# Loads in runs of one token, a chunk's state one step later, and half of the second group's first layer by twenty products, in a gated-recurrence and SiLU-MLP kernel on Trainium2

## The chip, the cores and the metric

The kernel runs on one core of one Trainium2 chip. The metric is the time of one execution in device microseconds: before the change 556.75 us, the median of three runs (555.87 to 556.92). All of the profile is of one further execution, which took 557.26 us; the span from its first to its last instruction is 555.5 us, with TensorE's granted clock at 0.999.

## The reference

A gated linear recurrence over 4 batches, 8 heads, 768 tokens and 48 dimensions a head, and then a two-layer block with SiLU on the 3072 rows of 384 that it gives. All is float32.

```python
for t in range(S):                                   # B, H, S, D = 4, 8, 768, 48
    state = alpha[:, :, t, :, None] * state + einsum('bhd,bhe->bhde', k[:, :, t], v[:, :, t])
    y[:, :, t] = einsum('bhd,bhde->bhe', q[:, :, t], state)
x = y.transpose(0, 2, 1, 3).reshape(B * S, H * D)    # 3072 x 384
h = x @ w_in                                         # 384 x 2048
out = (h * (1.0 / (1.0 + exp(-h)))) @ w_out          # 2048 x 384
```

## The kernel before

**Chunks and steps.** The recurrence is cut into 24 chunks of 128 tokens: chunk n is piece n // 4 of batch n % 4. For a chunk the kernel needs, per head, running products of alpha along the tokens (two scans on VectorE, L734 for u and L764 for p), `kp = k * u` (L749, L751) and `qp = q * p` (L770, written over p), a 128 x 128 matrix of scores `kp^T qp` on TensorE (L388, ps_a<-p,kp), which ScalarE copies out (L818, L821) and GpSimd masks to its causal half (L825), values from scores and v and from the carried state (ps_a<-g,vn and ps_a<-p,st), and the new state from kn and v (ps_a<-vn,kn), added on VectorE (L880). kn is kp turned: tokens on the partitions.

The loop at the end of `quotients` runs over steps. A step has four slots; the table `stages` says which parts of which chunk stand in a slot: in the later half (from step NA = 8) scores of chunk n-1 in slot 0, products of chunk n in slot 1 (alpha's turn, u, k's turn, kp), quotient in slot 2 (p, q's turn, qp), values and states of chunk n-1 and the flip of chunk n in slot 3. After each slot `fill` adds work of the two-layer block. TensorE's order is that of the program; the order on the other engines is settled by the scheduler that builds the kernel, save where `keep_in_program_order` is called.

**How a chunk gets in.** In the first eight steps a, k and q are loaded with tokens on the partitions and turned by TensorE. From chunk 8 on they are loaded into three tiles at, kt and qt (one each) in a form in which VectorE can turn them in blocks of 32 x 32: partition b of a block of 32 holds, for each head, four tokens in a row, 4b to 4b + 3, in one run of 768 bytes; a second load of the same data stands 32 floats further left on the next 32 partitions, so that dimensions 32 to 47 come to lie where the turn of the second half finds them. `turned` (L708) reads 32 floats for each token and writes every fourth float of its target, because of the token order. Each of the three loads is 4 DMAs on SP's queue (L486), issued when the turn of the chunk before has freed the tile.

**kn.** `flip` turns kp on VectorE (L780) into a tile `turn`, which also holds k's and q's turned forms, and stores it to DRAM (L782); `land` loads it back as kn, by 4 DMAs on SP's queue (L790), at the start of the next step.

**The two-layer block.** 3072 rows are six groups of 512; a group has two halves h of 256 rows (two chunks each). xt holds a half's rows turned. The first layer makes 16 blocks of 128 columns, in two pairs of 8 blocks: `pair` 0 and 1. Groups 0 and 1 take it plainly (`enter_plain`): for 2 blocks at a time 6 matmuls of 256 columns into a PSUM bank, and a SiLU by ScalarE (L923). Groups 2 to 5 take it by `enter`: 20 products of combined blocks for both halves together in place of 24, two matmuls each, in seven pieces; ScalarE copies PSUM banks out (L950), VectorE combines them (L958 and L587), ScalarE takes SiLUs of pairs of blocks (L955). Such products need 11 sums of token blocks (`sums_x`, tile xc) for each group, and 23 sums of w_in's blocks (`sums_w`, in w_in and a tile wx) for each pair, once. The second layer (`leave`) makes each half's output by 7 products, each 8 matmuls of 192 columns into ps_o, after a side-by-side sum of SiLU blocks (`side_by_side`, L1033) and differences (L1047); GpSimd's queue stores the result (L1059).

**Pieces.** `pieces` lists all pieces with a weight (12) and the chunk up to which values must be there; `fill` takes as many as are due by a schedule of marks. For group 1, pair 1 there are eight plain pieces, interleaved with the seven of `leave(0, 1)`. `done` inside `leave` also calls `sums_w`: pair 0 in `leave(0, 1)`, pair 1 in `leave(1, 0)`, four sums a piece.

PSUM: three banks for the first layer (ps_m), two for the second (ps_o), three for the recurrence (ps_a).

Of the kernel before, what the change touches and what calls it, by code (L numbers as in the profile page):

```python
# [9 lines left out]
I32 = mybir.dt.int32  # L10
# [345 lines left out]
def quotients(  # L356
# [109 lines left out]
    def load(n, names="akq"):  # L466
        if n == NT:
            return
        c = ctxs.setdefault(n, dict(zip(("ci", "b"), divmod(n, B))))
        b, rows = c["b"], slice(c["ci"] * C, c["ci"] * C + C)  # L470
        for name, src in (("a", alpha), ("k", k), ("q", q)):
            if name not in names:
                continue
            x = src[b, :, rows, :]
            if n < NA:
                c[name] = nat[name][n % NIN]
                nc.sync.dma_start(c[name][:, :, 0:D], x.transpose([1, 0, 2]))
                continue

            c[name] = late["quads"][name]
            for u in range(2):
                for i in range(2):
                    r = 64 * u + 32 * i
                    nc.sync.dma_start(  # L486
                        c[name][r : r + 32, 32 * (1 - i) :][:, 0 : 4 * NP * D].rearrange(
                            "p (g c) -> p g c", g=NP),
                        x[u::2].rearrange("h (b j) d -> b h (j d)", j=4))

    NV = 2
    vns = [fix.tile([128, H, 64], F32, name=f"vn{i}") for i in range(NV)]
# [164 lines left out]
    def audit():  # L657


        flat = alpha.rearrange("b h s d -> (b h s d)").rearrange("(p c) -> p c", p=128)  # L660
        assert 2 * HD <= 32 + 4 * NP * D
        todo = [(flat[:, c : c + AW], AW, 0) for c in range(0, flat.shape[1], AW)]
        if wide:
            todo += [(moe_w_in[t * 128 : t * 128 + 128, c : c + 512], 512, 1)
                     for c in range(0, DF, 512) for t in range(NKT)]
            todo += [(moe_w_out[f * 128 : f * 128 + 128, :], HD, 1) for f in range(NFT)]
        alone = sum(2 * x[1] > 32 + 4 * NP * D or x[2] == 0 for x in todo)
        for kind in (0, 1):
            n = sum(x[2] == kind for x in todo)
            if n:  # L670
                seen.append([fix.tile([128, n], F32, name=f"seen{kind}{i}") for i in range(2)])
        at = [0, 0]
        landed = []

        def begin(src, n, kind):
            at = len(landed)
            t = late["look"].tile([128, 512, 2], I32, name="bits").rearrange("p n w -> p (n w)") if (
                at < alone) else late["quads"]["akq"[at % 3]].bitcast(I32)
            if kind == 0:
                landed.append(t[:, 0:n].bitcast(F32))  # L680
                nc.sync.dma_start(landed[-1], src)
            else:
                nc.sync.dma_start(t[:, 0 : 2 * n], src.bitcast(I32))
                landed.append(t[:, 0 : 2 * n].rearrange("p (n w) -> p n w", w=2)[:, :, 1])

        for i, (src, n, kind) in enumerate(todo):

            while len(landed) < min(i + (1 if i + 1 < alone else 3), len(todo)):
                begin(*todo[len(landed)])
            x = landed[i]  # L690
# [13 lines left out]
        return t[:, 1 : NP * W + 1].rearrange("p (j c) -> p j c", c=W)[:, :, 0:C]  # L704

    def turned(x, to):
        x = x[:, 32:].rearrange("p (g j d) -> p g j d", j=4, d=D)
        dve.transpose(to.rearrange("p g (b j) -> p g j b", j=4), x[:, :, :, 0:32])  # L708

    def products(n):  # L710

# [70 lines left out]
        nc.sync.dma_start(c["flip"], t.rearrange("p c j d -> p (c j d)"))  # L782

    def land(n):
        c = ctxs[n]
        if "flip" in c:
            c["kn"] = work.tile([128, NP, C], F32, name="kn")
            x = c.pop("flip").rearrange("(r d) (i x) -> i d r x", r=4, i=4)
            for i in range(4):
                nc.sync.dma_start(c["kn"][32 * i : 32 * i + 32], x[i])  # L790

    def scores(n):
        c = ctxs[n]
# [117 lines left out]
    def enter_plain(grp, h, pair):  # L911

        if h == 0:
            g_tiles(grp, pair)
        xt = xts[2 * grp + h]
        for f in range(8 * pair, 8 * pair + 8, 2):
            ps = bank(f // 2 % 3).rearrange("p (e n) -> p e n", e=2)
            for e in range(2):
                for t in range(NKT):
                    pe.matmul(ps[:, e, :], lhsT=w_in[:, t, (f + e) * 128 : (f + e + 1) * 128],  # L920
                              rhs=xt[:, t, :], start=(t == 0), stop=(t == NKT - 1))
            q, i = divmod(f, 4)
            act.activation(gts[grp, h, pair][:, i : i + 2, q % 2, :], ps, AF.Silu)  # L923
            if grp == 1 and pair == h == 0:
                differences(f // 2)
                differences(4 + f // 2)
            if grp > 0 and f % 8 == 6:
                side_by_side(grp, h, pair)
            yield

    def enter(grp, pair):
        g_tiles(grp, pair)
        halves = [gts[grp, h, pair] for h in range(2)]

# [95 lines left out]
    def side_by_side(grp, h, pair):  # L1030

        x = cells(grp, h, pair, 1, 0)
        dve.tensor_tensor(x, x, cells(grp, h, pair, 1, 1), ALU.add)  # L1033

    def leave(grp, h):
# [26 lines left out]
        steps = iter(range(7))  # L1062

        def done():
            if 2 * grp + h in (1, 2):
                sums_w(2 * grp + h - 1, 4 * next(steps) + 4)

        def new(i):
            return out_bank(i, HO)
# [51 lines left out]
    def plain(grp, h, pair):  # L1121
        return (enter_plain(grp, h, pair), 12, 2 * (2 * grp + h) + 2)

    def group(grp):
        return [[(enter(grp, pair), 12, GB * grp + GB)] * 7 for pair in range(2)]

    def output(grp):
        return [[(leave(grp, h), 12, GB * grp + GB)] * 7 for h in range(2)]
# [9 lines left out]
    pieces += [plain(1, 0, 0)] * 4 + [(leave(0, 0), 12, GB)] * 7  # L1138
    phases = [len(pieces)]
    pieces += [plain(1, 1, 0)] * 4  # L1140
    both([(leave(0, 1), 12, GB)] * 7, [plain(1, 0, 1)] * 4 + [plain(1, 1, 1)] * 4)
    phases.append(len(pieces))
    before = output(1)
    for grp in range(2, NG):
# [13 lines left out]
    def go_on():  # L1158

        nonlocal done  # L1160
        next(pieces[done][0], None)
        done += 1

    audits = audit()
    done, bridged = 0, 0
    STEPS = NT + 1
    SLOTS = 4
# [3 lines left out]
    def settle():  # L1171

        first.close()
        late.update(look=pool("look"), part=pool("part"), turn=pool("turn"),
                    xc=pool("xc").tile([128, len(SUMS_X), TB], F32, name="xc"),
                    wx=pool("wx").tile([128, 8, NQ, 128], F32, name="wx"))
        quads = pool("quads")
        late["p"] = pool("p").tile([128, NP * W + 1], F32, name="p")
        late["quads"] = {name: quads.tile([128, 32 + 4 * NP * D], F32, name=f"{name}t") for name in "akq"}
        for name, t in late["quads"].items():  # L1180
            gps.memset(t, 1.0 if name == "a" else 0.0)
        load(NA)
# [20 lines left out]
    for step in range(STEPS):  # L1203
        if step == 1:
            load(NIN)
        stages = [[(scores, 1)], [(products, 0)], [(values, 1)], [(states, 1)]]
        if step == 1:

            stages = stages[1::-1] + stages[2:]
        elif step >= NA:  # L1210
            stages = [[(land, 1), (scores, 1)], [(products, 0)], [(quotient, 0)],
                      [(values, 1), (states, 1), (flip, 0)]]
        for slot, group in enumerate(stages):
            for stage, lag in group:
                n = step - lag
                if not 0 <= n < NT:
                    continue
                stage(n)
                if stage is values:
                    bridged = n + 1  # L1220
                if stage is states and n + 1 + NIN < NA:
                    load(n + 1 + NIN)
                if stage is states and n + NV < NT:
                    load_v(n + NV)
            if step * SLOTS + slot == (NA + 1) * SLOTS - 1:
                x = decayed.rearrange("p (o i c) -> p o i c", o=2, c=C)
                for r, o in later:
                    gps.memset(x[r, o, :, 0:CH], 0.0)
# [85 lines left out]
```

## Time and profile before

| | |
|---|---|
| median of three runs | 556.75 us |
| profiled execution | 557.26 us |
| its span | 555.5 us |
| TensorE matmul, busy | 541.4 us, 5026 records |
| VectorE, busy | 445.4 us, 801 instructions |
| ScalarE, busy | 208.5 us |
| GpSimd, busy | 76.1 us |
| first-layer record of 256 columns, from start to start | 0.216 us |
| turn by VectorE, L708, mean | 1.11 to 1.14 us, 48 in all |
| flip by VectorE, L780, mean | 0.71 us, 12 in all |
| issue of one load on SP's queue, L486, median | 0.43 us |
| chunk 9's scores on TensorE | at 143.83 us |
| chunk 12's scores | at 192.4 us |
| chunk 13's scores | at 213.8 us |

PE is TensorE, PEld its weight loads, DVE VectorE, ACT ScalarE, POOL GpSimd, SP the engine whose queue issues most DMAs. A float32 matmul stands as two records. A line of a timeline has the start in us, the time from its first start to its last end, engine, line, operation, output<-inputs, shape and count; in brackets the idle time of the engine before it and what ended that. A line of the view of waits reads: who waited <- for whom: us in total, times, longest. A DVE instruction of 128 x 512 shows as 0.69 us and one of 128 x 256 as 0.42, but the next one starts after 0.61 and 0.34: their ends overlap. xcount in a group is the number of instructions.

### The profile page before, as it was taken

The numbers are of one execution on the slowest core, as the hardware profiler recorded it, in microseconds if no ns is written. First come the engines' busy times: TensorE is split into PE (matmuls) and PEld (weight loads), VectorE is DVE, ScalarE is ACT, GpSimd is POOL, SyncE is SP. The second block draws the span as 40 slices with busy tenths as digits, with TensorE's granted clock in tenths as the row PEclk, the third lists the DMA queues.
The fourth block names the chain that finished last, engine by engine and source line by source line (L and its number), as shares of the span: only waits on it lengthen the run. The fifth ranks groups of instructions, "written<-read, shape, count | busy, mean of one in ns | idle before, by whom it ended". The sixth has DMA issues, their size and how long they took to land. (4 is left out here: it accounts for less than half of the span.)

```text
span 555.5 us, 12640 instructions
## 1 busy us (share of the span) xinstructions
PE 541.4 (97%) x5026; PEld 489.7 (88%) x5026; DVE 445.4 (80%) x801; ACT 208.5 (38%) x466; POOL 76.1 (14%) x146
## 2 busy tenths in 40 slices
PE   6999999999999999999999999999999999999996
PEld 4788887998899999899999999988998999999996
DVE  5897788974999899997998986998884796945431
ACT  2556653223333253353353353344263342332100
POOL 3210000222210212021011021021121000001000
PEclk9999999999999999999999999999999999999999
DMA  9998971164454625355545654617642135500000
GB/s 215 246 249 210 232 195 33 47 161 116 117 136 125 159 63 138 86 145 149 139 112 139 193 139 120 191 27 183 170 137 91 54 91 169 172 11 22 10 24 30
DMA packets 99217, 70.09 MB, mean 126 GB/s; under 512 B 56272, under 2 KB 88656, under 8 KB 99152
## 3 DMA queue, kind: packets, MB, share of 16 engines
q1 hardware_dynamic: 97232, 65.30, 45.1%
q0 software_dynamic: 1920, 3.93, 2.0%
q8 instruction: 40, 0.66, 0.5%
q14 instruction: 25, 0.20, 0.1%
HBM read 61.34 MB, written 7.86 MB: 125 GB/s over the span
## 5 line engine op out<-in xcount | busy, mean ns | idle before, releaser
L388 PE MATMUL ps_o<-w_out,g 128*128 128x192 f32 x768 | 134.0, 328 | 0.5 <-DVE o L1056 0.5
L388 PEld LDWEIGHTS ps_o<-w_out,g 128*128 128x128 f32 x768 | 125.6, 190 | 3.5 <-DVE o L1056 1.0
L388 PE MATMUL ps_m<-xt,w_in 128*128 128x256 f32 x480 | 113.6, 383 | 1.5 <-ACT xt L863 1.1
L388 PEld LDWEIGHTS ps_m<-xt,w_in 128*128 128x128 f32 x480 | 89.1, 190 | 14.4 <-ACT xt L863 1.6
L388 PE MATMUL ps_o<-wt,g 128*128 128x192 f32 x576 | 99.7, 326 | 0.0
L388 PEld LDWEIGHTS ps_o<-wt,g 128*128 128x128 f32 x576 | 95.1, 190 | 1.6 <-issue 0.2
L388 PE MATMUL ps_m<-xc,w_in 128*128 128x256 f32 x288 | 70.7, 382 | 0.0
L388 PEld LDWEIGHTS ps_m<-xc,w_in 128*128 128x128 f32 x288 | 53.7, 190 | 7.0 <-DVE g L958 0.3
L1047 DVE TENSOR_TENSOR g<-g 128x512 f32<-128x512 f32 x72 | 50.1, 709 | 8.3 <-PE ps_o L388 8.3
L955 ACT ACTIVATE g<-g 128x1024 f32<-128x1024 f32 x32 | 33.1, 1056 | 61.2 <-DVE g L958 61.1
L1059 POOL DMA_DIRECT2D out_dram<-o x40 | 22.0, 551 | 219.5 <-DVE o L1056 113.7
L825 POOL TENSOR_SCALAR_AFFINE_SELECT g<-g 64x256 f32<-64x256 f32 x64 | 34.9, 546 | 124.4 <-ACT g L818 105.7
L388 PE MATMUL ps_m<-xc,wx 128*128 128x256 f32 x192 | 50.1, 383 | 1.0 <-DVE xc L586 1.0
L950 ACT COPY g<-ps_m 128x512 f32<-128x512 f32 x64 | 36.6, 588 | 37.0 <-PE ps_m L388 36.9
L388 PEld LDWEIGHTS ps_m<-xc,wx 128*128 128x128 f32 x192 | 35.2, 190 | 5.2 <-ACT u L1078 1.2
L958 DVE TENSOR_TENSOR g<-ps_m,g 128x512 f32<-128x512 f32 x56 | 37.1, 683 | 3.2 <-PE ps_m L388 2.7
L734 DVE TENSOR_TENSOR_SCAN u<-al,one 128x516 f32<-128x516 f32 x24 | 29.8, 1240 | 11.9 <-ACT al L731 11.6
L923 ACT ACTIVATE g<-ps_m 128x512 f32<-128x512 f32 x32 | 19.1, 597 | 41.7 <-PE ps_m L388 41.4
L950 ACT COPY part<-ps_m 128x512 f32<-128x512 f32 x32 | 18.9, 590 | 38.0 <-PE ps_m L388 24.0
L697 DVE TENSOR_REDUCE seen<-bits 128x1 f32<-128x512 int32 (+1 forms) x33 | 26.3, 823 | 5.7 <-DMA bits<-in_moe_w_in_dram 5.7
L764 DVE TENSOR_TENSOR_SCAN p<-al,inv 128x516 f32<-128x516 f32 x24 | 29.9, 1247 | 1.0 <-PE ps_a L388 0.3
L1056 DVE TENSOR_TENSOR o<-ps_o,u 128x192 f32<-128x192 f32 x24 | 8.5, 355 | 25.7 <-PE ps_o L388 22.8
(129 smaller groups left out, 648.5 us busy)
## 6 DMA issues: line engine op xcount, KB each, us to landing
bits<-in_moe_w_in_dram SPq DMA_DIRECT2D x24, 512.0 KB, 4.7
bits<-in_moe_w_out_dram SPq DMA_DIRECT2D x16, 384.0 KB, 3.9
at<-in_alpha_dram SPq DMA_DIRECT2D x64, 96.0 KB, 2.5
kt<-in_k_dram SPq DMA_DIRECT2D x64, 96.0 KB, 2.6
qt<-in_q_dram SPq DMA_DIRECT2D x64, 96.0 KB, 2.7
bits<-in_alpha_dram SPq DMA_DIRECT2D x9, 512.0 KB, 4.0
out_dram<-o POOLq DMA_DIRECT2D x40, 96.0 KB, 2.4
flips<-turn SPq DMA_DIRECT2D x12, 256.0 KB, 2.4
```

The source lines that it names most:

```text
L388: in_order(nc.tensor.matmul(*args, **kw))
L697: dve.tensor_reduce(seen[kind][which][:, i : i + 1], x, axis=AX, op=op, apply_absolute_value=True))
L734: dve.tensor_tensor_scan(u[:, end - 1 :: -1], sg[:, end:0:-1], one[:, end:0:-1], 0.0, ALU.mult, ALU.add)
L764: dve.tensor_tensor_scan(p[:, 0:end], sg[:, 0:end], iv[:, 0:end], 0.0, ALU.mult, ALU.add)
L825: gps.affine_select(x, x, pattern=[[0, NP], [1, CH]], compare_op=ALU.is_ge, fill=0.0, base=0, channel_multiplier=-1)
L923: act.activation(gts[grp, h, pair][:, i : i + 2, q % 2, :], ps, AF.Silu)
L950: act.copy(to, ps)
L955: act.activation(x, x, AF.Silu)
L958: dve.tensor_tensor(to, a, b, op)
L1047: dve.tensor_tensor(cells(grp, h, pair, *to), cells(grp, h, pair, *x), cells(grp, h, pair, *y), ALU.subtract)
L1056: dve.tensor_tensor(o, x, y, ALU.add)
L1059: (gps if grp < NG - 1 else nc.sync).dma_start(out[r : r + C, c * HO : (c + 1) * HO], o)
```

## The change

Four things are changed.

- at, kt and qt hold tokens in another order. Partition b holds, for each head, tokens b, 32 + b, 64 + b and 96 + b, each in a run of its own of 192 bytes: 8 DMAs of 32 x 4 x 48 floats for each tensor in place of 4 of 32 x 4 x 192, each datum loaded once. The second 32 partitions get dimensions 32 to 47 by a copy on ScalarE (`beside`), two for each tensor. The turn then writes neighbouring floats.
- `land` issues kn's loads on GpSimd's queue, one step later, and `states` stands a step later too, with v's load for the chunk after next behind it.
- Group 1, pair 1 is taken by `enter` (20 products for both halves) in place of eight plain pieces, so `sums_x(1)` is needed, and pair 1's sums of w_in are made beside `leave(0, 0)` (three a piece) and the plain pieces of group 1's second half (four a piece), pair 0's in `leave(1, 0)`. Group 2 takes pair 1 before pair 0.
- The side-by-side sum after a plain piece is issued after the piece that follows it (`owed`).

```diff
@@ load
             c[name] = late["quads"][name]
-            for u in range(2):
-                for i in range(2):
-                    r = 64 * u + 32 * i
-                    nc.sync.dma_start(
-                        c[name][r : r + 32, 32 * (1 - i) :][:, 0 : 4 * NP * D].rearrange(
-                            "p (g c) -> p g c", g=NP),
-                        x[u::2].rearrange("h (b j) d -> b h (j d)", j=4))
+            for g in range(NP):
+                for u in range(2):
+                    nc.sync.dma_start(c[name][64 * u : 64 * u + 32, g],
+                                      x[2 * g + u].rearrange("(j b) d -> b j d", b=32))
+
+    def beside_q(n):
+        beside(n, "q")
+
+    def beside(n, names="ak"):
+        for name in names if NA <= n < NT else "":
+            for u in range(2):
+                r = slice(64 * u, 64 * u + 32)
+                act.copy(ctxs[n][name][64 * u + 32 : 64 * u + 64, :, :, 0 : D - 32],
+                         ctxs[n][name][r, :, :, 32:D])
@@ turned
-        x = x[:, 32:].rearrange("p (g j d) -> p g j d", j=4, d=D)
-        dve.transpose(to.rearrange("p g (b j) -> p g j b", j=4), x[:, :, :, 0:32])
+        dve.transpose(to.rearrange("p g (j b) -> p g j b", j=4), x[:, :, :, 0:32])
@@ land
-        c = ctxs[n]
+        c = ctxs.get(n, {})
...
-                nc.sync.dma_start(c["kn"][32 * i : 32 * i + 32], x[i])
+                gps.dma_start(c["kn"][32 * i : 32 * i + 32], x[i])
@@ enter_plain, enter
+            if grp == h == 1:
+                sums_w(1, sums_done[1] + 4)
             if grp > 0 and f % 8 == 6:
-                side_by_side(grp, h, pair)
+                owed.append((done, grp, h, pair))
...
     def enter(grp, pair):
+        sums_w(pair, len(SUMS_W))
@@ leave: done
-            if 2 * grp + h in (1, 2):
-                sums_w(2 * grp + h - 1, 4 * next(steps) + 4)
+            if grp == h == 0 and late:
+                sums_w(1, sums_done[1] + 3)
+            if grp == 1 and h == 0:
+                sums_w(0, 4 * next(steps) + 4)
@@ pieces
+    def second(grp, pair):
+        return [(enter(grp, pair), 12, GB * grp + GB)] * 7
+
     def group(grp):
-        return [[(enter(grp, pair), 12, GB * grp + GB)] * 7 for pair in range(2)]
+        return [second(grp, pair) for pair in ((1, 0) if grp == 2 else (0, 1))]
...
-    both([(leave(0, 1), 12, GB)] * 7, [plain(1, 0, 1)] * 4 + [plain(1, 1, 1)] * 4)
+    pieces += [(sums_x(1), 0, 2 * GB)] * 2
+    both([(leave(0, 1), 12, GB)] * 7, second(1, 1))
@@ go_on
         next(pieces[done][0], None)
+        while owed and owed[0][0] < done:
+            side_by_side(*owed.pop(0)[1:])
         done += 1
@@ stages, from step NA on
-            stages = [[(land, 1), (scores, 1)], [(products, 0)], [(quotient, 0)],
-                      [(values, 1), (states, 1), (flip, 0)]]
+            stages = [[(beside, 0), (scores, 1)], [(land, 2), (beside_q, 0), (products, 0)],
+                      [(quotient, 0)], [(values, 1), (states, 2 if step > NA else 1), (flip, 0)]]
```

What is left out here: the tiles at, kt and qt lose their 32 spare columns (768 floats a partition in place of 800), and the checks of sizes that go with that.

More of the change, by code (lines that the diff above doesn't have):

```diff
@@ L660, in audit @@
         flat = alpha.rearrange("b h s d -> (b h s d)").rearrange("(p c) -> p c", p=128)
-        assert 2 * HD <= 32 + 4 * NP * D
+        assert 2 * HD <= 4 * NP * D
         todo = [(flat[:, c : c + AW], AW, 0) for c in range(0, flat.shape[1], AW)]
@@ L666, in audit @@
             todo += [(moe_w_out[f * 128 : f * 128 + 128, :], HD, 1) for f in range(NFT)]
-        alone = sum(2 * x[1] > 32 + 4 * NP * D or x[2] == 0 for x in todo)
+        alone = sum(2 * x[1] > 4 * NP * D or x[2] == 0 for x in todo)
         for kind in (0, 1):
@@ L677, in begin @@
             t = late["look"].tile([128, 512, 2], I32, name="bits").rearrange("p n w -> p (n w)") if (
-                at < alone) else late["quads"]["akq"[at % 3]].bitcast(I32)
+                at < alone) else late["quads"]["akq"[at % 3]].rearrange(
+                    "p g j d -> p (g j d)").bitcast(I32)
             if kind == 0:
@@ L1161, in go_on @@
         next(pieces[done][0], None)
+        while owed and owed[0][0] < done:
+            side_by_side(*owed.pop(0)[1:])
         done += 1
     audits = audit()
+    owed = []
     done, bridged = 0, 0
@@ L1178, in settle @@
         late["p"] = pool("p").tile([128, NP * W + 1], F32, name="p")
-        late["quads"] = {name: quads.tile([128, 32 + 4 * NP * D], F32, name=f"{name}t") for name in "akq"}
+        late["quads"] = {name: quads.tile([128, NP, 4, D], F32, name=f"{name}t") for name in "akq"}
         for name, t in late["quads"].items():
@@ L1215, in quotients @@
                 n = step - lag
-                if not 0 <= n < NT:
+                if not 0 <= n < NT or (stage is states and n == step - 2 < NA):
                     continue
```

## The prediction

> **What bounds the kernel now.** I read the engine totals first, then TensorE's waits, then the timeline around one wait.
>
> ```profile
> span 555.5 us, 12640 instructions
> PE 541.4 (97%) x5026; PEld 489.7 (88%) x5026; DVE 445.4 (80%) x801; ACT 208.5 (38%) x466; POOL 76.1 (14%) x146
> ...
> PE ps_m L388 <- DVE xc L586: 1.0, 1, 1.0
> PE ps_a L388 <- DVE p L770: 0.5, 1, 0.5
> PE ps_m L388 <- DVE g L958: 0.4, 1, 0.4
> ...
> 203.76 1.89 PE L388 MATMUL ps_m<-xc,w_in 128*128 128x256 f32 x8
> 205.49 1.03 PE L388 MATMUL ps_m<-xt,w_in 128*128 128x256 f32 x4
> 206.35 2.76 PE L388 MATMUL ps_o<-wt,g 128*128 128x192 f32 x16
> 209.05 1.08 PE L388 MATMUL ps_a<-g,vn 128*32 128x128 f32 x32
> ```
>
> TensorE is never without work from about 24 us to the end; its waits in between are a handful of half microseconds. In the stretch shown, twelve 256-column records take 206.35 - 203.76 = 2.59 us, 0.216 each, and sixteen 192-column ones 2.70. So time falls only by matmuls taken away or waits taken away, and rises by every wait put before a matmul. VectorE (80%, over 14 of each 15 us from 150 to 180 and from 195 to 255) is what makes TensorE wait: all three waits quoted end on it.
>
> The place that matters most, in the vector queue and TensorE's own:
>
> ```profile
> 130.34 1.23 DVE L764 TENSOR_TENSOR_SCAN p<-al,inv 128x516 f32<-128x516 f32 x1
> 139.21 0.69 DVE L1033 TENSOR_TENSOR g<-g 128x512 f32<-128x512 f32 x1 [7.63 <-ACT g L923]
> 139.82 1.13 DVE L708 STREAM_TRANSPOSE turn<-kt 128x512 f32<-128x512 f32 x1
> ...
> 141.85 1.11 DVE L708 STREAM_TRANSPOSE turn<-qt 128x512 f32<-128x512 f32 x1
> 142.99 0.69 DVE L770 TENSOR_TENSOR p<-turn,p 128x512 f32<-128x512 f32 x1
> 143.72 0.71 DVE L780 STREAM_TRANSPOSE turn<-kp 128x512 f32<-128x512 f32 x1
> ...
> 140.48 2.87 PE L388 MATMUL ps_o<-w_out,g 128*128 128x192 f32 x16
> 143.83 0.90 PE L388 MATMUL ps_a<-p,kp 48*64 48x128 f32 x32 [0.48 <-DVE p L770]
> ```
>
> The side-by-side sum (L1033) waits 7.63 us for the last SiLU of a plain piece; k's and q's turns and the product p of chunk 9 stand behind it; the scores of chunk 9 wait for p.
>
> [...] the L1033 above holds a turn whose data had landed. [...] The turn at L708 writes every fourth float (16 bytes apart) and takes 1.13 us; the turn at L780 writes neighbours and takes 0.71. [...]
>
> **The change, part by part.**
>
> *Twenty products for group 1's second half.* Out: 2 x 4 plain pieces of 6 matmuls, 48; in: 20 x 2 = 40. A float32 matmul is two records: 16 x 0.216 = **-3.46 us** of TensorE. It adds to VectorE 14 combinations x 0.69 (L958) = 9.7 and 11 token sums x 0.44 (the xc rows) = 4.9, and to ScalarE 12 copies x 0.59 + 4 SiLUs x 1.06 - 8 plain SiLUs x 0.60 = 6.5 us.
>
> *Runs of one token.* The turn now writes neighbours: 48 x (1.13 - 0.71) = -20.2 us of VectorE, 1.3 in each of 16 steps. No row shows just this turn; L780 is nearest. If the gap on the reading side (32 of 48 floats) is what costs, the gain is nothing, so 0 to 1.3 a step; I take 1.3, since L780 reads in blocks too. Price: 6 copies a step on ScalarE, 96 in all; nearest are L818 (256 elements, 0.376) and L821 (128, 0.263): 0.38 each, 36.5 us, hidden by a ScalarE at 38% unless one stands before a copy that empties PSUM while its load is out. SP: 24 loads + 3 of v + 1 flip, 28 issues where there were 20, each 0.43 (at, median): 12.0 us a step. The shortest step, from scores 10 to scores 11, loses one of its five pieces: 176.2 - 160.0 = 16.2 less 2.6 is 13.5 us, so SP still fits, with little over.
>
> *kn by GpSimd, states a step later.* 48 issues x 0.55 (out_dram's row) = 26.4 us on POOL, before the masks of the next scores. The masks feed values, a good half step later; POOL is 14% busy: nothing. Without that cover, 2.2 us a step. The flip has then been written for a step: no wait. The four state products move from before scores 9 to later, 0.45 us of displacement that comes back.
>
> *Sums of w_in.* The 23 sums of the second half (0.34 apart) go into the 7.63 us hole above and before it; those of the first half take their place in the next group. The changed VectorE queue between chunk 8's alpha turn and L1033 gains 20 sums, 7.6 us, less two alpha turns, k's and q's gain: it ends near 137-138, before 139.2. Covered.
>
> *Scores 9.* Behind L1033 the changed queue has three token sums and three w_in sums more before p. Before, L1033 to the end of p took 143.68 - 139.21 = 4.47; after, 4.47 + 6 x 0.38 - 2 x 0.42 = 5.9, so p ends at 145.1. L1033 itself cannot move, since TensorE's pieces before it are the same. TensorE arrives at 143.83 - 0.48 - 0.45 = 142.9 and waits 2.35 us instead of 0.48: **+1.9**. All that follows on TensorE starts later by as much; VectorE and ScalarE follow TensorE's pieces there and lose nothing more.
>
> *Scores 12.* The new products end in step 11. In the changed VectorE queue both side-by-side sums of that half and k's turn stand before p of chunk 12. From the last product: 0.85 to the last combination, two SiLUs (2.0 to 2.25 together, from half a microsecond on), second sum 0.65, kp 0.78, two state adds 0.72, q's turn 0.73, p 0.69, in all 6.6 to 6.9, with VectorE 0.4 late: 7.2. TensorE has 361.12 - 356.22 = 4.9 us of work in the same place of a later step (values, states, eight output matmuls). So it waits 7.2 - 4.9 = 2.3 to 2.4 us: **+2.4**. In the kernel before, this step ended in a plain piece, with 2.2 us of chain.
>
> *Step 13.* p of 13 stands 1.9 us ahead of TensorE where it stood 213.8 - 210.65 = 3.1; the fourth, sixth and seventh pieces' reads of PSUM come late by 0.35, 0.3 and 0.6 us, where one wait of 0.4 stood: **+0.8**.
>
> *Later steps.* VectorE is lighter by 1.3 us a step, p comes over half a step early, and the token sums that held TensorE at 368.38 (1.0 above, 0.96 in the timeline) come in time: **-0.96**. Start and tail are unchanged.
>
> Sum: -3.46 + 1.9 + 2.4 + 0.8 - 0.96 = **+0.7 us**. On the profiled execution (557.26, span 555.5) that is 557.9 and 556.2; the median shown is 0.5 below that execution: **557.4 us**.
>
> **Rivals.** A measurement of this kernel cannot tell less than about 0.2% (1.1 us) from no change.
>
> A, above: the products' gain is paid out again at scores 9 and 12. 556.0 to 558.6, by 0.5 us of error at each of three waits. Chance 0.40.
>
> B, faster: the two waits do not come, because VectorE reaches p earlier than the queue order and these spacings say. Then -3.46 - 0.96, and up to 1 more where VectorE's relief removes small waits: 551.5 to 555, **553.3**. For it: the scheduler put those rows there as harmless. Against: the 7.63 us wait is set by TensorE's own pieces. Chance 0.20.
>
> C, slower by ScalarE: [...] a copy of a run that waits for eight landings holds the PSUM copies behind it. It decides when a load lands later than the copy's turn, in steps 9 to 12, where SP needs 12.0 of 13.5 us. With three banks in flight a late copy costs what it exceeds a piece (2.6 us) by; 1 us in each of four steps over A: **561.4**. Against: landing takes 2.5 us, and loads are issued most of a step ahead. Chance 0.22.
>
> D, slower by VectorE: the turns do not get faster (the change does not do what it says), or the thin margins at scores 8, 10 and 11 (about 1.0, 1.4, 0.6 us) are used up: 1.5 to 2 us over A, **559.2**. Chance 0.18.
>
> **Numbers.** Range 553.0 to 562.0: it leaves out the lower half of B and the upper end of C. A's own range is 556.0 to 558.6. Faster: B and a little of A, 0.22. Same: most of A, 0.36. Slower: C, D and A's upper part, 0.42.
>
> **What would show it.** Turns of at, kt and qt near 0.71; a wait of TensorE on p of about 2.4 us near 145 and another near 192; no wait on xc near 368; POOL with 26 us more; ScalarE near 251 us busy. Wrong if those two waits are missing (B), if ScalarE's rows show long waits for loads with TensorE waiting for ScalarE (C), or if the turns stay at 1.1 (D).

## The result, and the profile after

The changed kernel took 558.53 us (median of 22 executions, 556.32 to 561.42), the kernel before 556.90 (22 executions, 555.87 to 558.23). The ratio is 1.0027, 95% interval 1.0017 to 1.0037: slower by 0.9 to 2.1 us. The forecast was 557.4 in a range of 553.0 to 562.0, with slower by over 0.2% as the likeliest of the three outcomes. The total is close; the sum behind it is not, as the trace shows: two of its terms were too dear, one did not come, and two costs were missing.

The profiled execution took 560.03 us, 1.5 above its median. First the head of its page:

```profile
span 558.2 us, 13236 instructions
...
PE 538.6 (96%) x5010; PEld 486.7 (87%) x5010; DVE 440.2 (79%) x826; ACT 254.0 (46%) x570; POOL 105.3 (19%) x194
```

Then the changed operations among its groups of instructions (busy us, mean ns of one, idle time before them and what ended it):

```profile
L798 POOL DMA_DIRECT2D kn<-flips x48 | 26.2, 553 | 40.3 <-PE ps_a L388 34.5 <-DMA flips<-turn 5.7 <-issue 0.2
...
L496 ACT COPY kt<-kt 32x256 f32<-32x256 f32 x32 | 12.9, 403 | 16.7 <-DMA kt<-in_k_dram 13.0 <-DVE u L742 1.9 <-DVE u L1103 1.1
...
L716 DVE STREAM_TRANSPOSE turn<-qt 128x512 f32<-128x512 f32 x16 | 11.3, 708 | 0.5
L716 DVE STREAM_TRANSPOSE al<-at 128x512 f32<-128x512 f32 x16 | 11.3, 704 | 4.1 <-ACT at L496 3.9
```

The parts have their predicted prices: turns of 0.70 to 0.71 us, GpSimd 26.2 us for kn (26.4 expected), ScalarE 254 us (251 expected). New is the idle time: copies at L496 wait 13.0 us for k's loads, and an alpha turn waits 3.9 us for a copy. TensorE's waits in the changed kernel (total, times, longest):

```profile
PE ps_a L388 <- DVE p L778: 3.1, 2, 1.7
...
PE ps_m L388 <- DVE g L969: 2.1, 2, 1.9
...
PE ps_a L388 <- ACT xt L871: 0.7, 1, 0.7
```

The wait on the token sums near 368 is gone, and two waits on p have come. They are where the forecast put them. The timeline around scores 9 and scores 12, VectorE and TensorE rows:

```profile
139.88 0.69 DVE L1044 TENSOR_TENSOR g<-g 128x512 f32<-128x512 f32 x1 [2.82 <-ACT g L931]
...
140.49 0.42 DVE L590 TENSOR_TENSOR xc<-xt 128x256 f32<-128x256 f32 x1
...
144.53 0.68 DVE L778 TENSOR_TENSOR p<-turn,p 128x512 f32<-128x512 f32 x1
...
145.35 0.90 PE L388 MATMUL ps_a<-p,kp 48*64 48x128 f32 x32 [1.67 <-DVE p L778]
...
187.46 0.69 DVE L1044 TENSOR_TENSOR g<-g 128x512 f32<-128x512 f32 x1 [0.52 <-ACT g L966]
...
188.70 0.65 DVE L1044 TENSOR_TENSOR g<-g 128x512 f32<-128x512 f32 x1
...
191.32 0.69 DVE L778 TENSOR_TENSOR p<-turn,p 128x512 f32<-128x512 f32 x1
...
192.06 0.90 PE L388 MATMUL ps_a<-p,kp 48*64 48x128 f32 x32 [1.47 <-DVE p L778]
```

p of chunk 9 ends at 145.2 (145.1 predicted), behind a side-by-side sum that waited for its SiLU. TensorE waits 1.67 us there and 1.47 at scores 12; measured as the interval between matmuls less the usual one, 1.84 and 1.63.

Two stalls were in no term of the sum. The first, near 309 (VectorE, TensorE and SyncE rows):

```profile
302.50 0.38 SPq L690 DMA_DIRECT2D bits<-in_alpha_dram  x1
...
306.62 1.22 DVE L706 TENSOR_REDUCE seen<-bits 128x1 f32<-128x1024 f32 x1 [2.28 <-DMA bits<-in_alpha_dram]
307.75 0.68 DVE L969 TENSOR_TENSOR g<-g,part 128x512 f32<-128x512 f32 x1
...
308.35 0.68 DVE L969 TENSOR_TENSOR g<-ps_m,g 128x512 f32<-128x512 f32 x1
...
309.09 1.13 PE L388 MATMUL ps_m<-xt,wx 128*128 128x256 f32 x4 [1.93 <-DVE g L969]
```

The kernel also checks the range of its inputs: it loads alpha and the weights a second time (tile `bits`) and reduces them on VectorE (L706). Here that reduction stands in VectorE's queue and waits for a load that SyncE issued at 302.50, between loads of k, v and alpha. The combination that empties TensorE's bank stands behind it. The second, near 342:

```profile
341.54 0.43 PE L388 MATMUL ps_a<-p,kp 48*64 48x128 f32 x2
341.75 0.40 ACT L496 COPY kt<-kt 32x256 f32<-32x256 f32 x1 [4.97 <-DMA kt<-in_k_dram]
...
342.17 0.48 ACT L871 COPY xt<-ps_a 128x384 f32<-128x384 f32 x1
...
342.70 0.89 PE L388 MATMUL ps_a<-p,kp 48*64 48x128 f32 x30 [0.73 <-ACT xt L871]
```

ScalarE holds a copy of k for 4.97 us until its loads land; the copy that empties TensorE's PSUM tile stands behind it. k's eight loads had been issued from 335.26 to 340.2, right after k's turn. In both, the instruction behind began only as the one that waited ended: the combination at 308.35 reads products that had ended by 303.7, and xt's copy products that had ended by 338.5. In the kernel before, k's turn at 139.82 stood likewise behind the sum that waited 7.63 us, and its loads had landed by 124.7.

One more link stands before both stalls. k's turned form is written into the same single tile `turn` as the flip of the chunk before, and the flip's store to DRAM still reads it (VectorE and SyncE rows):

```profile
329.87 0.43 SPq L790 DMA_DIRECT2D flips<-turn  x1
...
334.48 0.71 DVE L716 STREAM_TRANSPOSE turn<-kt 128x512 f32<-128x512 f32 x1 [1.76 <-DMA at<-in_alpha_dram]
...
335.26 4.96 SPq L485 DMA_DIRECT2D kt<-in_k_dram  x8
```

The store landed 4.5 us after its issue, at 334.36. k's turn began 0.12 us later, with VectorE idle for 1.76 us, although the last copy of its data had ended at 321.6; only then were the next loads of k issued. Ahead of the first stall the store landed at 293.97 and the turn began at 293.99, and SyncE issued k's loads before the load that the range check waits for. In 6 of 12 chunks of this kernel k's turn begins within 0.25 us of that landing; in the kernel before it never begins less than 1.5 us after it. The profile names another DMA for the wait, and no run gave the tile a second buffer, so what this link costs is not shown.

Last, the end. Between the start of the last matmul and the end of the span lie 6.1 us; before, 5.1. SyncE's waits, in the kernel after and in the kernel before, at the branch that ends the program:

```profile
SPq L1302 <- SPq L1302: 2.6, 1, 2.6
```

```profile
SPq L1282 <- SPq L1282: 1.7, 2, 1.2
```

After the branch SyncE stands 2.6 us before its next instruction; in the kernel before it stood 0.5, and then 1.2 for the last store.

Time by stretches, from the trace: us between the first score matmuls of the chunks named, then to the start of the last matmul, then to the end of the span. "Again" is the second profiled execution of the changed kernel (below).

| kernel | 8 to 9 | 9 to 12 | 12 to 14 | 14 to 17 | 17 to 20 | 20 to 23 | 23 to last | end |
|---|---|---|---|---|---|---|---|---|
| before | 14.2 | 48.6 | 42.9 | 63.3 | 62.5 | 63.6 | 125.8 | 5.1 |
| after | 15.0 | 46.7 | 42.0 | 63.4 | 65.8 | 63.1 | 125.8 | 6.1 |
| after, again | 15.0 | 46.9 | 42.1 | 63.9 | 64.5 | 62.7 | 125.8 | 6.1 |
| runs of one token alone | 13.8 | 48.6 | 41.9 | 63.3 | 64.4 | 62.8 | 125.8 | 6.1 |
| twenty products alone | 15.6 | 46.9 | 46.1 | 63.3 | 62.5 | 63.7 | 125.8 | 5.1 |
| sums later | 14.0 | 47.2 | 42.5 | 63.3 | 62.6 | 62.7 | 125.8 | 6.1 |
| v by GpSimd | 13.3 | 45.2 | 44.1 | 65.2 | 62.5 | 62.7 | 125.8 | 6.1 |

From scores 8 to scores 17 the changed kernel gains 1.9 us (again: 1.1). It gives back 3.3 (2.0) between scores 17 and 20 and 1.0 at the end.

### The profile page after: what moved, and what is told of

Read it like the earlier page. It is cut to its first block, busy times and chain, and to the rows that moved or that the text cites. A ratio compares the mean times of both kernels' runs of the same rounds, so it can differ in the third digit from the quotient of the medians.

```text
span 558.2 us, 13236 instructions
## 1 busy us (share of the span) xinstructions
PE 538.6 (96%) x5010; PEld 486.7 (87%) x5010; DVE 440.2 (79%) x826; ACT 254.0 (46%) x570; POOL 105.3 (19%) x194
## 5 line engine op out<-in xcount | busy, mean ns | idle before, releaser
L388 PE MATMUL ps_m<-xt,w_in 128*128 128x256 f32 x396 | 94.4, 382 | 1.1 <-ACT xt L871 1.1
L388 PEld LDWEIGHTS ps_m<-xt,w_in 128*128 128x128 f32 x396 | 73.6, 190 | 11.7 <-ACT xt L871 1.6
L388 PE MATMUL ps_m<-xc,w_in 128*128 128x256 f32 x324 | 79.6, 382 | 0.0
L388 PEld LDWEIGHTS ps_m<-xc,w_in 128*128 128x128 f32 x324 | 60.4, 190 | 7.6
L388 PE MATMUL ps_m<-xc,wx 128*128 128x256 f32 x216 | 56.4, 383 | 0.0
L961 ACT COPY g<-ps_m 128x512 f32<-128x512 f32 x72 | 41.0, 588 | 29.7 <-PE ps_m L388 29.2
L969 DVE TENSOR_TENSOR g<-ps_m,g 128x512 f32<-128x512 f32 x63 | 41.9, 683 | 5.0 <-PE ps_m L388 4.2
L388 PEld LDWEIGHTS ps_m<-xc,wx 128*128 128x128 f32 x216 | 39.5, 190 | 4.5 <-issue 0.2
L961 ACT COPY part<-ps_m 128x512 f32<-128x512 f32 x36 | 21.2, 590 | 40.1 <-DVE g L969 23.2
L798 POOL DMA_DIRECT2D kn<-flips x48 | 26.2, 553 | 40.3 <-PE ps_a L388 34.5
L706 DVE TENSOR_REDUCE seen<-bits 128x1 f32<-128x512 int32 (+1 forms) x33 | 26.5, 823 | 7.6 <-DMA bits<-in_alpha_dram 4.2
L388 PEld LDWEIGHTS ps_a<-p,kp 48*64 48x64 f32 (+1 forms) x640 | 20.9, 148 | 11.1 <-issue 6.3
```

The source lines that it names most:

```text
L388: in_order(nc.tensor.matmul(*args, **kw))
L798: gps.dma_start(c["kn"][32 * i : 32 * i + 32], x[i])
L961: act.copy(to, ps)
L969: dve.tensor_tensor(to, a, b, op)
```

## The experiments

Two theories were tested. S: the products' gain is paid out at scores 9 and 12, because side-by-side sums stand ahead of p. L: the runs of one token lose time in the late steps, because loads arrive late, by SyncE's queue or by ScalarE's order. Each result is a median with its ratio to the kernel before, timed beside it (556.9 to 557.3). The changed kernel was timed twice, 558.53 us (ratio 1.0027) and 559.26 (1.0032, the last run below). "Over the changed kernel" counts from the first; against the second the excess is 0.7 us smaller, so an excess of less than 1 us is not clear of noise.

### The two halves of the change apart

The kernel before with the loads, the copies on ScalarE, kn by GpSimd and the later states, but plain pieces and sums as they were. The line that decides (the others put the calls of the sums back):

```
-    both([(leave(0, 1), 12, GB)] * 7, second(1, 1))
+    both([(leave(0, 1), 12, GB)] * 7, [plain(1, 0, 1)] * 4 + [plain(1, 1, 1)] * 4)
```

> The kernel before with the runs of one token alone (loads, copies on ScalarE, kn by GpSimd, states a step later); group 1 stays in plain pieces and the sums of w_in stay where they were. Theory L (the late steps lose to loads that arrive late): the stalls of 2.1 us near 309 and 1.0 near 342 belong to this part, less the 1.0 of the wait on xc near 368 and the 0.6 before scores 9 that go: about +1.5 us, 558.4 by a before of 556.9. Rival S (everything that is lost comes from the twenty products and their sums): this part alone gains the two waits that go, -1.5 us, 555.4.

Measured: 557.67 us, ratio 1.0013 (1.0005 to 1.0022), +0.7 us, between the two. Its trace has a stall of 0.73 us at 308.0 and one of 0.91 at 341.6, so both belong to this half of the change. The wait before scores 9, which both theories here took to go, is still there (0.5). It also has the 6.1 us at the end.

The reverse, the twenty products and the moved sums on the kernel before (again the lines that decide):

```
-    both([(leave(0, 1), 12, GB)] * 7, [plain(1, 0, 1)] * 4 + [plain(1, 1, 1)] * 4)
+    pieces += [(sums_x(1), 0, 2 * GB)] * 2
+    both([(leave(0, 1), 12, GB)] * 7, second(1, 1))
```

> The kernel before with the twenty products for group 1's second half and the moved sums alone; the turns stay at 1.13 us. Theory S: k's and q's turns stand before p of chunk 9 and of chunk 12, so the waits there are 0.84 longer than in the changed kernel, 2.7 and 2.5 us, against 3.46 of products and the 0.6 of wait that stood before scores 9: +1.1 us, 558.0. If those waits come only with the other part of the change, this gains the products: 553.5.

Measured: 560.54 us, ratio 1.0063 (1.0046 to 1.0079), +3.5. The direction is that of S, the size is not. Scores 9 waits 2.1 us, but the large loss is between scores 12 and 14: 46.1 us where the kernel before takes 42.9. The timeline there, VectorE and TensorE rows (in this kernel L708 is the turn, L961 the combination):

```profile
217.32 1.11 DVE L708 STREAM_TRANSPOSE al<-at 128x512 f32<-128x512 f32 x1
...
218.26 0.71 DVE L880 TENSOR_TENSOR st<-ps_a,st 48x192 f32<-48x192 f32 x2
...
219.00 1.45 DVE L734 TENSOR_TENSOR_SCAN u<-al,one 128x516 f32<-128x516 f32 x1
...
220.49 0.69 DVE L961 TENSOR_TENSOR g<-ps_m,g 128x512 f32<-128x512 f32 x1
...
221.23 1.13 PE L388 MATMUL ps_m<-xt,wx 128*128 128x256 f32 x4 [0.92 <-DVE g L961]
```

VectorE, which has turns of 1.1 us and the sums of w_in in this stretch, reads TensorE's banks late: stalls of 0.9 us at 205.6, 1.1 at 221.2, 0.6 at 232.6 and two of 0.4. The two halves do not add: +0.7 and +3.5 alone, +1.6 together. With twenty products in place the runs of one token gain 2.0 us (560.54 to 558.53); without them they lose 0.7.

### The sums behind p

The side-by-side sum of group 1's last plain pieces is put two pieces later and kept there in program order; of the two sums that end the new products, the second one is put behind as well (`pin` keeps the program order):

```
-        for h in range(2):
-            side_by_side(grp, h, pair)
+        side_by_side(grp, 0, pair)
+        owed.append((done + 1 if grp == 1 else done - 1, grp, 1, pair))
...
-        while owed and owed[0][0] < done:
-            side_by_side(*owed.pop(0)[1:])
+        while owed and owed[0][0] + (2 if owed[0][1:] == (1, 1, 0) else 0) < done:
+            side_by_side(*owed.pop(0)[1:], pin=True)
```

> The changed kernel with two side-by-side sums moved behind p: that of group 1's last plain pieces behind p of chunk 9, and that of the second pair's second half behind p of chunk 12. Theory S: the wait of 1.84 us before scores 9 goes, that of 1.63 before scores 12 falls by 0.7: -2.5 us, 556.0. Rival (the waits only move, since VectorE has the same work to do before the first products on xc): 558.5.

Measured: 555.57 us, ratio 0.9974 (0.9965 to 0.9983): 3.0 us less than the changed kernel, and faster than the kernel before. S holds in kind, by less than expected: the waits shrank to 0.8 and 1.3 us, which is 1.3 of the 3.0. What is left at scores 9 is not the sum's. Chunk 8's flip was done at 128.45, and its store stood on SyncE's queue behind loads of k, q and v:

```profile
137.08 0.55 SPq L790 DMA_DIRECT2D flips<-turn  x1
...
139.75 0.71 DVE L716 STREAM_TRANSPOSE turn<-kt 128x512 f32<-128x512 f32 x1 [3.35 <-DMA at<-in_alpha_dram]
```

The store landed at 139.38, and k's turn began 0.37 us later (in the kernel before it landed at 131.39, 8.4 us ahead of the turn). So of the 1.84 us at scores 9 the sum explains 1.0; by these times the rest comes from a late transfer too.

The rest of the gain fits the late stalls: this kernel's profiled execution has none near 309 or 342. k's copy waited nearly as long, but TensorE came later than it:

```profile
337.77 0.40 ACT L496 COPY kt<-kt 32x256 f32<-32x256 f32 x1 [4.26 <-DMA kt<-in_k_dram]
338.19 0.48 ACT L871 COPY xt<-ps_a 128x384 f32<-128x384 f32 x1
...
338.60 0.86 PEld L388 LDWEIGHTS ps_a<-p,kp 48*64 48x64 f32 x32 [0.33 <-DVE al L716]
338.60 1.02 PE L388 MATMUL ps_a<-p,kp 48*64 48x128 f32 x32
```

### Which queue makes the loads late

k alone back in runs of four tokens (four loads, a turn of 1.13 us, no copies); the loads, with the turn and the tile's shape changed back likewise:

```
+            if name in "k":
+                for u in range(2):
+                    for i in range(2):
+                        r = 64 * u + 32 * i
+                        nc.sync.dma_start(
+                            c[name][r : r + 32, 32 * (1 - i) :][:, 0 : 4 * NP * D].rearrange(
+                                "p (g c) -> p g c", g=NP),
+                            x[u::2].rearrange("h (b j) d -> b h (j d)", j=4))
+                continue
```

> The changed kernel with k alone loaded and turned as before (runs of four tokens, four loads, no copy on ScalarE, a turn of 1.13 us). Theory L by ScalarE (a copy of k that waits for its loads holds back the copy that empties PSUM): the 1.0 us near 342 goes and others of its kind, about -1 us, 557.5; the stall near 309, where VectorE waits for a load that SyncE issued late, may shrink by up to 2 us, since SyncE has four issues a step less: 555.5 to 557.5. Rival: VectorE, 0.42 us a step heavier, is what binds: 558.5 or above.

Measured: 560.34 us, ratio 1.0069 (1.0053 to 1.0086), +1.8 over the changed kernel. The stalls near 309 and 342 are gone (17 to 20 takes 62.5), as L expected of four issues and two copies less. But k's turn stands in the chain to p: the waits before scores 9 and 12 are 2.1 and 2.3 us, and a stall of 1.1 has come at 276. The sum came out as the rival, VectorE, expected.

ScalarE's copies of k behind the copies of the scores (and kept in program order there):

```
-            stages = [[(beside, 0), (scores, 1)], [(land, 2), (beside_q, 0), (products, 0)],
+            stages = [[(beside_a, 0), (scores, 1)], [(land, 2), (beside_kq, 0), (products, 0)],
```

> The changed kernel with ScalarE's two copies of k put behind the copies of the same step's scores, instead of ahead of them. Theory L by ScalarE: the stall of 1.0 us near 342, where the copy that empties PSUM stood behind a copy of k that waited 5.0 us for its loads, goes; the one near 309 stays: -1 us, 557.5. Rival: k's copy is late because SyncE issues eight loads one after the other, and the wait only moves to k's turn on VectorE and so to kp and the next scores: 558.5 or more.

Measured: 559.56 us, ratio 1.0046 (1.0031 to 1.0062), +1.0 over the changed kernel and only 0.3 over its second timing, which is not clear of noise. The stall near 342 is gone, and others are there: 1.0 at 274.4, 0.8 at 284.1, 0.9 at 402.0. VectorE's turns now wait for k's copies, 4.6 us in five times. That fits the rival: the order on ScalarE decides who waits for the late load.

All copies by GpSimd:

```
-                act.copy(ctxs[n][name][64 * u + 32 : 64 * u + 64, :, :, 0 : D - 32],
+                gps.tensor_copy(ctxs[n][name][64 * u + 32 : 64 * u + 64, :, :, 0 : D - 32],
```

> The changed kernel with all six copies of a step that shift the runs done by GpSimd instead of ScalarE. Theory L by ScalarE's order (its copies waiting for loads hold back the copies that empty PSUM): the 1.0 us near 342 and smaller ones go, -1 to -1.5 us, 557.0 to 557.5. Rival: the masks of the scores now stand behind copies that wait for loads, and values wait for the masks; a step's copies are up to 5 us late in the trace: 560 to 570.

Measured: 560.51 us, ratio 1.0056 (1.0043 to 1.0069), +2.0 over the changed kernel (+1.3 over its second timing), the low end of what the rival expected. A copy takes 0.49 to 0.60 us on GpSimd where ScalarE takes 0.40, and 9 to 12 takes 48.4 us instead of 46.7. Whether the masks did it, as the rival says, was not told apart from the slower copies.

v's loads by GpSimd:

```
-        nc.sync.dma_start(t[:, 0 : H // 2, 0:D], x[:, 0 : H // 2])
+        gps.dma_start(t[:, 0 : H // 2, 0:D], x[:, 0 : H // 2])
         for e in range(2):
-            nc.sync.dma_start(t[CH * e : CH * e + CH, H // 2 :, 0:D], x[CH - CH * e : C - CH * e, H // 2 :])
+            gps.dma_start(t[CH * e : CH * e + CH, H // 2 :, 0:D], x[CH - CH * e : C - CH * e, H // 2 :])
```

> The changed kernel with the three loads of v of a step issued by GpSimd instead of SyncE (on SyncE they stand ahead of loads of k, alpha and of the range check). Theory L by SyncE's queue: the loads behind them come about 1.5 to 2 us earlier, the stalls near 309 (2.1, VectorE waiting for a load of the range check) and near 342 (1.0) go: -2.5 us, 556.0. Rival: those two stalls are chance, the loss is at scores 9 and 12 alone: 558.5; if GpSimd's masks come late instead: 559 or more.

Measured: 556.11 us, ratio 0.9995 (0.9976 to 1.0014), 2.4 less than the changed kernel: the expected number, for another reason. The scheduler that builds the kernel placed VectorE's instructions anew, and p of chunks 9 and 12 now stands ahead of the side-by-side sums. Around scores 12, VectorE and TensorE rows:

```profile
183.19 0.67 DVE L778 TENSOR_TENSOR p<-turn,p 128x512 f32<-128x512 f32 x1
...
186.20 0.67 DVE L1044 TENSOR_TENSOR g<-g 128x512 f32<-128x512 f32 x1
...
187.13 0.69 DVE L1044 TENSOR_TENSOR g<-g 128x512 f32<-128x512 f32 x1
...
188.65 0.90 PE L388 MATMUL ps_a<-p,kp 48*64 48x128 f32 x32
```

No wait is left at either place. From scores 9 to 12, with no wait at either end, this kernel takes 45.2 us and the kernel before 48.6: that is the whole of the products' gain. It agrees with S, but SyncE's relief is in it too: without v's loads ahead of it, the store of chunk 8's flip was issued at 133.37 and landed at 135.47 (139.99 in the changed kernel), k's turn began at 135.79, and p could stand ahead of the sum. The stalls near 309 and 342 are gone, but one of their kind, a copy of k that waited 4.6 us for its loads, has come at 256 (1.7 us), and one of 1.8 at 221, where sums of w_in stand ahead of a combination. So this run does not settle L.

kn by SyncE, as it was before the change:

```
-                gps.dma_start(c["kn"][32 * i : 32 * i + 32], x[i])
+                nc.sync.dma_start(c["kn"][32 * i : 32 * i + 32], x[i])
```

> The changed kernel with kn's four loads of a step on SyncE again instead of GpSimd; all else as changed. Theory L by SyncE's queue: SyncE has 32 issues a step instead of 28, some 2 us more, so what stands behind them (k's and q's loads) comes later and TensorE waits more in the steps after 14: 559.5 to 561.5. Rival (GpSimd's issuing of kn was worth nothing): 558.5; where the two state adds, which fall behind p of chunk 12 here, are taken off the wait before scores 12: 558.1.

Measured: 562.70 us, ratio 1.0092 (1.0074 to 1.0111), +4.2 over the changed kernel (+3.4 over its second timing), more than L expected. Its profiled execution takes 3.7 us longer than the changed kernel's between scores 9 and 12, where TensorE waits for the landing of kn itself (timeline near 191):

```profile
185.26 0.56 SPq L790 DMA_DIRECT2D flips<-turn  x1
185.87 1.88 SPq L798 DMA_DIRECT2D kn<-flips  x4
...
191.44 0.41 PEld L388 LDWEIGHTS ps_a<-vn,kn 128*32 128x32 f32 x32 [2.91 <-DMA kn<-flips]
191.44 0.55 PE L388 MATMUL ps_a<-vn,kn 128*32 128x48 f32 x32 [2.64 <-DMA kn<-flips]
```

The last of the four loads was issued at 187.3, behind loads of k, q and v and a flip, and landed at 191.4. Four more issues a step cost this kernel 3.4 to 4.2 us: SyncE's queue has little room left. GpSimd's part of the change, priced at nothing, is what makes the rest bearable. For one DMA the issue is the smaller part: in the changed kernel one of k's loads takes 0.43 us to issue and 2.0 from there to its landing (medians). For eight in a row it is not: issuing k's eight took 3.7 us at best and 5.0 ahead of the stall near 342.

### Together, and once more

The later sums with v by GpSimd:

> Both the later side-by-side sums (555.6 alone) and v's loads by GpSimd. The sums' kernel shows no stalls near 309 and 342, so theory L expects little from the second edit here in most executions, but less scatter: 554.5 to 555.6, fewer executions above 556. Rival (GpSimd's masks come late): 556 or more.

Measured: 555.67 us, ratio 0.998 (0.9966 to 0.9993), as the later sums alone (555.57); the scatter, 555.14 to 559.16, is not smaller. What scores 9 and 12 gain, stalls of 0.65 and 1.5 us at 214 and 221 take.

The later sums with three sums of w_in a piece instead of four:

```
-                sums_w(0, 4 * next(steps) + 4)
+                sums_w(0, 3 * next(steps) + 3)
```

> The two later side-by-side sums (555.6 alone), and three instead of four sums of w_in after each output piece of group 1's first half. VectorE's queue from step 13 on has fewer sums ahead of the combinations that empty TensorE's banks: the stall of 0.4 us near 227 goes and the last sums fall into step 15: 554.8 to 555.6. Rival: sums pushed to the end hold up the first products of the next half, 556.5 or more.

Measured: 555.07 us, ratio 0.9957 (0.9943 to 0.9972), the lowest median here, faster than the kernel before by 2.0 us by the medians and by 2.4 by the ratio; its interval overlaps that of the later sums alone (0.9965 to 0.9983). The stall near 227 is gone, but a copy of k again held TensorE up, by 0.8 us at 338.1. Its TensorE waits, in the same view as above:

```profile
PE ps_a L388 <- DVE p L778: 1.9, 2, 1.2
...
PE ps_a L388 <- ACT xt L871: 0.6, 1, 0.6
```

All three edits:

> Later side-by-side sums, three sums of w_in a piece, and v's loads by GpSimd. With v's loads there, p of chunks 9 and 12 stood ahead of TensorE and two stalls of 0.65 and 1.5 us came near 214 and 221, where sums of w_in stand before the combinations; with two of the four moved behind, about 1 us of that goes: 554.6 by a median of 555.7. Rival: the stall only moves with the sums: 555.7.

Measured: 556.53 us, ratio 0.9993 (0.9982 to 1.0003), 1.5 us above the two edits without v's loads. The stall at 221 fell from 1.5 to 0.8 us, as expected, but at 255 a copy of k held TensorE up by 2.3: a late load again, at another place.

The changed kernel once more:

> The changed kernel once more, for a second profiled execution. If the stalls of 2.1 us near 309 and 1.0 near 342 are set by the order of SyncE's and ScalarE's queues, they stand at the same places with sizes within 1 us; if they are chance, they are gone or elsewhere. The waits before scores 9 and 12 stand at 1.8 and 1.6 in either case.

Measured: 559.26 us, ratio 1.0032 (1.0016 to 1.0049). Its waits on p are as before, and both late stalls stand at their places, 0.9 us at 308.3 and 0.8 at 341.7; one of 0.6 at 273.4 is new. The first shrank by 1.2, a little more than the 1 us allowed. So, as far as two executions show, the places are set by the kernel and the sizes vary with the execution.

```profile
PE ps_a L388 <- DVE p L778: 3.3, 2, 1.7
...
PE ps_m L388 <- DVE g L969: 0.8, 1, 0.8
...
PE ps_a L388 <- ACT xt L871: 0.6, 1, 0.6
```

## Why the prediction was right, and where not

The side and the size were right (+1.6 measured, +0.7 forecast), but by luck: the errors of the sum cancel. By its steps:

- **Twenty products, -3.46.** Right. Where no wait stands at either end (v by GpSimd), scores 9 to 12 fell by 3.4 us.
- **Scores 9, +1.9.** The mechanism is right in part; the term measured +1.2. From the start of the side-by-side sum to the end of p took 5.3 us in both profiled executions, not 5.9: the two lighter turns gave 1.1 us there and not 0.84, and the six sums took 0.35 each and not 0.38. That p ended within 0.1 us of the forecast is luck: in step 8, taken as without cost, the first alpha turn waited 3.9 us for its copies, TensorE lost 0.6 us at 119 and 122, and sum, p and TensorE all came later by about as much. In the second execution p ended at 144.6, and the wait was the same. Nor does the sum explain all of it: without it 0.8 us stayed, because of the flip's store.
- **Scores 12, +2.4.** Right mechanism, measured 1.6 and 1.8. The chain from the last product (185.7) to the end of p (192.0) took 6.3 us, not 7.2: VectorE was not 0.4 late, and the parts that the forecast lists add up to 6.4 to 6.7, not to its 6.6 to 6.9.
- **Step 13, +0.8.** Did not come: 12 to 14 is 0.9 shorter than before. The lighter turns fit this: with slow turns (twenty products alone) the same stretch is 3.2 longer than before, though that kernel differs in the queues too. The forecast read late PSUM reads off the queue's order, and placed the relief of VectorE only in later steps.
- **Wait on the token sums, -0.96.** Gone; 20 to 23 is 0.5 to 0.9 shorter.
- **SyncE, "12.0 of 13.5".** The step that failed. The price of 0.43 an issue is its duration; in a row they start 0.47 us apart at the median, which makes 13.2 of the 13.5, and eight took 3.7 us at best and 5.0 ahead of the stall near 342. With the loads of the range check SyncE issued 362 DMAs between 150 and 380 us, 173 us of issuing in 230 (before: 240, 115 us). The margin was worked out for steps 9 to 12 alone, and as an average. What counts is a chain: the flip's store lands, k's turn runs and frees k's tile, eight loads are issued one after the other, the last lands, ScalarE copies, and only then the next turn (for the stall near 342: landing 334.36, turn 334.48, issues 335.26 to 340.2, copies 341.75 to 343.1, turn 347.12). In steps 17 to 20 that chain came out late for VectorE and ScalarE: TensorE stood for 0.8 to 2.1 us at a time, and the stretch grew by 2.0 to 3.3 us.
- **kn by GpSimd, nothing.** As priced for TensorE. What it was worth, 3.4 to 4.2 us, was not asked. "The flip has then been written for a step: no wait" did not hold: for chunk 8 GpSimd waited 5.7 us for the flip's store, and 6 of k's 12 turns behind such stores began within 0.25 us of a landing. The stores' time from issue to landing is 3.9 us at the median, before the change 2.4.
- **Tail unchanged.** Wrong by +1.0 us, in every kernel here with runs of one token, and not with the twenty products alone.

By stretches the second profiled execution reads, against the kernel before: +0.1 up to scores 8; -0.9 from there to scores 12, where the forecast had -3.46 + 1.9 + 2.4 = +0.8; -0.8 from 12 to 14 (forecast +0.8); +0.6 and +2.0 from 14 to 20 (forecast nothing); -0.9 from 20 to 23 (forecast -0.96); +1.0 at the end (forecast nothing). That is +1.1; the spans differ by 1.3, and the rest is rounding. So the changed part of the kernel came out 3.3 us better than forecast, and 3.6 us came from what had been taken as hidden.

Of the rivals, D fell (turns of 0.71). B named what the two waits are worth, and the kernels with later sums reach it in part: 555.07 against its 553.3. C's mechanism was real, in other steps than it named and as one of two forms: the copy of k ahead of a PSUM copy, and the range check's reduction ahead of a combination. That the late loads come with the half of the change that has the runs of one token is shown; that four issues more a step cost 3.4 to 4.2 us is shown by kn. That relief of SyncE alone removes the late stalls is not shown: moving v's loads also moved VectorE's order, and a late copy of k came up elsewhere. How the late stalls divide between the eight issues and the shared tile `turn` is open.

## What to carry to other kernels

When work is taken off the engine that bounds the kernel, look at what stands ahead of its next operand on the engine that finishes that work: two additions placed behind that operand instead of ahead of it turned a loss of 1.6 us into a gain of 1.5, 1.3 of it by the waits themselves. A load cut into more, smaller transfers is priced on the issuing queue, as a chain from the freed tile to the last landing in the tightest step, not as an average: here 28 issues of 0.43 us made 12.0 of 13.5 us, and k's eight alone took 5.0 ahead of a stall. The chain can begin with a store from a tile that is then written again: k's turn began within 0.25 us of the landing of the flip's store in 6 of 12 chunks, and chunk 8's flip waited 8.6 us for its store's issue with the later sums (2.0 in the kernel before). After any edit read the order of the other queues again: moving three loads of v to another engine changed VectorE's order at two places that decided the time.

## What the runs showed of the hardware

In the changed kernel SyncE's issues of alpha, k and q start 0.47 us apart in a row where one lasts 0.43 (medians); k's eight took 3.7 us at best and 5.0 ahead of the stall near 342. VectorE's turn of 128 x 512 takes 1.11 to 1.14 us when it writes every fourth float and 0.70 to 0.71 when it writes neighbours, though both read 32 of every 48 floats; with k alone in the old form, k's turns took 1.13 and the others 0.71 in one kernel. The branch at the end of the program cost SyncE 2.6 to 2.8 us in each kernel with runs of one token, and 0.5 without; part of it lies beside the landing of the last store (1.9 us after the branch in the changed kernel), and the end is 1.0 us longer. No run here shows the cause, and the stall does not grow with the number of issues: it was 2.6 us with 24 on SyncE a step (k in the old form), 28 and 32 (kn by SyncE).
